# Handing out operand tiles and PSUM areas in strict rotation in a one-core attention and feed-forward kernel

## The chip, the cores and the metric

The kernel runs on one core of one Trainium2 chip. The metric is the device time of one execution in microseconds (us). The core's engines work side by side, each through its own queue of instructions in order, and wait for each other by semaphores: PE (TensorE, matrix products into PSUM), ACT (ScalarE), DVE (VectorE), POOL (GpSimd), and SP, which issues the transfers.

## What is computed

Two stages follow each other. The first is an attention through 49 agents: the agents attend to all keys and values, and each query attends to the agents. The second takes the 24960 resulting rows of 128 numbers through a feed-forward layer with 2048 hidden units and a clipped quadratic gate.

```python
def sm(a, b):
    s = scale * (a @ b.transpose(0, 2, 1))
    ...
    e = np.exp(s)
    return e / (e.sum(-1, keepdims=True) + 1e-09)
a2k = sm(agents, k)            # B = 2, N = 12480, C = 128, 49 agents
agent_v = a2k @ v
q2a = sm(q, agents)
x = q2a @ agent_v              # 24960 rows
...
h = x @ w_in                   # 128 -> 2048
g = np.where(h >= 1, h, np.where(h <= -1, 0.0, (h + 1) ** 2 / 4))
return g @ w_out               # 2048 -> 128
```

## The kernel before

The 24960 rows are cut into 49 tiles of 512. The 2048 hidden units are cut into eight pairs of 128-row blocks, so each tile has eight pairs, and a pair goes through these steps (function `pair`):

- `g1`: PE multiplies the tile's softmax weights `mt` (49 rows, kept as a high and a low part) with weights that already hold the agents' values times `w_in` (`w_hi`, `w_lo`), into a PSUM area `ph` of 128x1024. Six products (L1208).
- `relu` (L1216) and `square` (L1221): ACT writes `g = relu(0.5 h + 0.5)` from `ph`, then squares `g` in place.
- `gate` (L1224): DVE combines `g` and `ph` into the gated value, in place in `g`. After it `ph` is free.
- For six of the eight pairs `hi` (a rounded copy, `ghi`, L356 on POOL or L358 on DVE) and `lo` (the rest, `glo = g - ghi`, L1235, on POOL or DVE). After `lo` the tile `g` is free. Then PE adds `ghi` times `wo_hi` and `wo_lo`, and `glo` times `wo_hi`, into `total` (L1248).
- For the other two pairs PE multiplies `g` itself with `wo` (L1248, `total<-g,wo`), and `g` is free after that.

Between the pairs of a tile stand the query scores of a later tile (L1080, into a `ph` area), their softmax on DVE and ACT, the transposes of the result (L1127), and the output's evacuation (L354 `ot`, L1297) and store. Before the first tile the keys and values of the first batch are worked through. Those of the second batch ride along in tiles 3 to 23: their products (L381 keys, L389 values, L1016 weights) are put behind the query scores in the same `ph` area, and ACT and DVE then evacuate them (L354 `ks`, `w_hi`; L397 to L400 `acc`).

The order of the instructions on every engine is fixed when the kernel is built. A planner (class `Order`) places all steps by times written in tables (`TIMES`, `START`). It counts buffers (`BUFS`: five of `g`, five of `ghi`, five of `glo`, three of `ph`), but it does not choose which of them a step gets. The choice is made when a step's function runs and asks a pool for a tile:

```python
hip = ctx.enter_context(tc.tile_pool(name="hi", bufs=BUFS["hi"]))
...
def new_h():
    return psh.tile([128, 2, 512], F32, name="ph", tag="ph")
...
def wide(pool, name, dtype):
    return pool.tile([128, 2, T], dtype, name=name, tag=name)[:, :, 0:n]
```

All buffers of a kind share one tag, and the pool's allocator picks one for each new tile. The first instruction that writes a new tile then waits for the last users of the tile that had this buffer before. At the start some buffers of `g`, `ghi` and `glo` are lent to transfers of keys and values.

Of the kernel before, what the change touches and what calls it, by code (L numbers as in the profile page):

```python
# [13 lines left out]
F32 = mybir.dt.float32  # L14
F32R = mybir.dt.float32r
# [7 lines left out]
T = 512  # L23
# [32 lines left out]
    hi=(1.9175717, 2.5099120, None, 1.9817459, None, 2.5080745, 2.9293395, 2.4146834),  # L56
    lo=(2.3736696, 2.6831976, None, 1.9174717, None, 2.7685071, 2.6705867, 2.1491229),
# [16 lines left out]
BUFS = dict(k=4, v=4, q=4, qs=3, m=2, g=5, hi=5, lo=5, o=2, wf=2, h=3, d=2, ex=1, t0=1, t1=1)  # L74
# [172 lines left out]
def agent_attention_moe(  # L247
# [33 lines left out]
    small = ctx.enter_context(tc.tile_pool(name="small", bufs=BUFS["qs"]))  # L281
    qp = ctx.enter_context(tc.tile_pool(name="q", bufs=BUFS["q"]))
    mp = ctx.enter_context(tc.tile_pool(name="m", bufs=BUFS["m"]))
    gp = ctx.enter_context(tc.tile_pool(name="g", bufs=BUFS["g"]))
    hip = ctx.enter_context(tc.tile_pool(name="hi", bufs=BUFS["hi"]))
    lop = ctx.enter_context(tc.tile_pool(name="lo", bufs=BUFS["lo"]))
    op = ctx.enter_context(tc.tile_pool(name="o", bufs=BUFS["o"]))
    wfp = ctx.enter_context(tc.tile_pool(name="wf", bufs=BUFS["wf"]))
    dp = ctx.enter_context(tc.tile_pool(name="d", bufs=BUFS["d"]))
    dxp = ctx.enter_context(tc.tile_pool(name="ex", bufs=BUFS["ex"]))  # L290
    psh = ctx.enter_context(
        tc.tile_pool(name="psh", bufs=BUFS["h"], space=bass.MemoryType.PSUM)
    )
    psx = ctx.enter_context(tc.tile_pool(name="psx", bufs=1, space=bass.MemoryType.PSUM))

# [54 lines left out]
    dve, act, pool = nc.vector, nc.scalar, nc.gpsimd  # L350

    def copy(engine, out, in_):
# [4 lines left out]
        else:  # L357
            dve.tensor_copy(out, in_)  # L358

    def new_h():  # L360
        return psh.tile([128, 2, 512], F32, name="ph", tag="ph")

    PS = {}

# [168 lines left out]
    def keys_phase(b, keep, k_key, v_key, s_key, m_key, a_key, e_key, p_key=0.0, wait=None):  # L533
# [11 lines left out]
        for g in range(NG):  # L545
            lent = "g" if g % 2 and g < 2 * BUFS["g"] else "k"
            kb = [] if lent == "g" else [kbuf[keep.pop(0)]]

            def fn(o, e, g=g, kb=kb, h=slice(0, KG * SUB)):
                if not kb:  # L550
                    x = gp.tile([128, 2, T], F32, name="g", tag="g")
                    kb.append(x.rearrange("p c t -> p (c t)")[:, 0:KG * SUB])
                nc.sync.dma_start(out=kb[0][:, h], in_=kT[b, :, g * KG * SUB:][:, h])

            rest = []
            if g:
                LK[g] = load(128 * KG * SUB * 4, fn, (), k_key(g), (lent,))
            else:
                n, m = HALF * SUB, KG * SUB
                LK[g] = load(  # L560
                    128 * n * 4, lambda o, e, fn=fn: fn(o, e, h=slice(0, n)), (), k_key(g) - 1.0,
                    ("k",),
                )
                rest = [load(
                    128 * (m - n) * 4, lambda o, e, fn=fn: fn(o, e, h=slice(n, m)), (), k_key(g)
                )]

            def scores(o, e, g=g, kb=kb, lo=0, hi=HALF):
                if lo == 0:
                    area(o, ("k", b, g))  # L570
                ps = one(PS["k", b, g])


                for t in range(lo, hi):
                    columns(
                        ps[:, t * A:t * A + A2], kb[0][:, t * SUB:(t + 1) * SUB], agf[:, 0:A2]
                    )

            def scores2(o, e, scores=scores):
                scores(o, e, lo=HALF, hi=KG)  # L580

            def evac(o, e, g=g):
                copy(
                    e, ksf[:, g, 0:KG * A],
                    one(PS[("k", b, g)] if g else PS.pop(("k", b, g)))[:, 0:KG * A],
                )

            def gm(o, e, g=g):
                f = top.rearrange("p t a -> p (t a)")
                dve.tensor_tensor(  # L590
                    out=f, in0=one(PS.pop(("k", b, g)))[:, 0:KG * A],
                    in1=f if g > 1 else ksf[:, 0, 0:KG * A], op=ALU.max,
                )

            def gm2(o, e, g=g):
                dve.tensor_reduce(
                    out=pms[part(g)], in_=top.rearrange("p t a -> p a t"), axis=AX.X, op=ALU.max
                )

            x = add(("PE", 0.134 * HALF), scores, [LK[g], ld_ag], s_key(g))  # L600
            back = take(x)
            y = add(
                ("PE", 0.134 * (KG - HALF)), scores2, [x, *rest], s_key(g), (), ((lent, LK[g]),)
            )
            x.rows = y.rows = 2
            KE[g] = add(
                elementwise("evac", KG * A), evac, [y, *([wait[g]] if wait else [])], s_key(g) + 1, (),
                () if g else (back,),
            )
            if g:  # L610
                KX[g] = add(
                    ("DVE", 0.42), gm, [KE[g], *([KX[g - 1]] if g > 1 else [])], s_key(g) + 1.1, (),
                    (back,),
                )
            if g + 1 in (*first_of, NG):
                KX[g] = add(("DVE", 0.69), gm2, [KX[g]], s_key(g) + 1.2)

        mb_ops, rescale = [], None
        for i in range(len(first_of)):
# [36 lines left out]
            key = m_key if i + 1 == len(first_of) else p_key  # L656
            x = add(("PE", 0.1), m2, [KX[end]], key + 0.1)
            back = take(x)
            mx_op = x = add(("DVE", 0.2), m3, [x], key + 0.2)
            x = add(("DVE", 0.15, 1), m4, [x], key + 0.3)  # L660
# [7 lines left out]
        for g in range(NG):  # L668

            lent = ("hi", "lo")[g % 2] if b == 0 and g < NLENT else "v"  # L670
            vb = [vbuf[(b * NG + g - NLENT) % BUFS["v"]]] if lent == "v" else []
            s = ks[:, g, 0:KG, :]

            def fn(o, e, g=g, vb=vb, lent=lent):
                if not vb:
                    x = (hip if lent == "hi" else lop).tile(
                        [128, 2, T], F32R, name="g" + lent, tag="g" + lent
                    )
                    x = x.bitcast(F32).rearrange("p c t -> p (c t)")[:, 0:KG * (C + 1)]
                    vb.append(x.rearrange("p (t c) -> p t c", c=C + 1))  # L680
                nc.sync.dma_start(out=vb[0], in_=v[b, :, g * KG:(g + 1) * KG, :])

            LV[g] = load(SUB * KG * (C + 1) * 4, fn, (), v_key(g), (lent,))

            def sub(o, e, s=s, mb=mbs[part(g)]):
                (pool if e == "POOL" else dve).tensor_tensor(
                    out=s, in0=s, in1=mb.unsqueeze(1).to_broadcast([SUB, KG, A]),
                    op=ALU.subtract,
                )

            def exp(o, e, s=s):
                f = s.rearrange("p t a -> p (t a)")
                act.activation(out=f, in_=f, func=ACTF.Exp, scale=scale)

            g0 = first_of[part(g)]
            count = ((first_of + [NG])[part(g) + 1] - g0) * KG
            ps = total[:, 0, part(g) * 256:][:, 0:256]

            def av(o, e, g=g, vb=vb, g0=g0, count=count, ps=ps, lo=0, hi=HALF):
                beside(ps, g, vb[0], lo, hi, (g - g0) * KG, count)  # L700

            def av2(o, e, av=av):
                av(o, e, lo=HALF, hi=KG)

            k = a_key(g)
            x = add(elementwise("sub", KG * A), sub, [mb_ops[part(g)], KE[g]], e_key(g))
            x = add(("ACT", 0.39), exp, [x], e_key(g) + 0.5)
            x = add(
                ("PE", 0.125 * HALF), av, [x, LV[g], *av_ops[-1:]], k, () if g else ("t0",)
            )  # L710
            if not g:
                av_ops.append(x)
            x.rows = 2
            x = add(("PE", 0.125 * (KG - HALF)), av2, [x], k, (), ((lent, LV[g]),))
            x.rows = 2
            av_ops.append(x)
            if (g - g0 + 1) * KG == count:
                def plus(o, e, ps=ps, first=not part(g)):
                    join_halves(o, ps, first)

                if part(g):
                    last = add(("DVE", 0.2), rescale[1], [rescale[0], last], k + 0.9)
                last = add(
                    ("DVE", 0.45), plus, [x] + ([last] if part(g) else []), k + 1, (),
                    (("t0", av_ops[0]),) if part(g) else (),
                )
# [457 lines left out]
    def pair(j, p, w_ops, wo_op):  # L1184
        st = {}
# [9 lines left out]
        hi_e, lo_e = plan(HI_ENG, j)[p], plan(LO_ENG, j)[p]  # L1195
        n = width(j)

        def wide(pool, name, dtype):
            return pool.tile([128, 2, T], dtype, name=name, tag=name)[:, :, 0:n]

        def g1(o, e):
            st["h"] = new_h()
# [24 lines left out]
            )  # L1227

        def hi(o, e):
            st["hi"] = wide(hip, "ghi", F32R)  # L1230
            copy(e, st["hi"], st["g"])

        def lo(o, e):
            st["lo"] = wide(lop, "glo", F32R)
            (pool if e == "POOL" else dve).tensor_tensor(  # L1235
                out=st["lo"], in0=st["g"], in1=st["hi"].bitcast(F32), op=ALU.subtract
            )
# [202 lines left out]
```

## Time and profile before

| | |
|---|---|
| time, median of 3 runs | 1073.84 us (1072.96 to 1073.86) |
| time of the profiled execution | 1073.93 us |
| its span, first to last instruction | 1072.2 us |
| PE busy | 1003.1 us, 94% |
| DVE busy | 921.2 us, 86% |
| ACT busy | 903.0 us, 84% |
| POOL busy | 632.4 us, 59% |
| granted TensorE clock, mean over the span | 0.994 |

The profiled execution's time is 1.7 us above its span; that part lies outside the instructions. The engines' shares are means over a start of some 64 us, in which the transfers are busy, and 49 tiles of about 20 us each. A share below 100% says that an engine waited or had nothing to do, not which of the two; the views of waits and of the timeline tell that.

### The profile page before, as it was taken

The numbers are of one execution on the slowest core, as the hardware profiler recorded it, in microseconds if no ns is written. First come the engines' busy times: TensorE is split into PE (matmuls) and PEld (weight loads), VectorE is DVE, ScalarE is ACT, GpSimd is POOL, SyncE is SP. The second block draws the span as 40 slices with busy tenths as digits, with TensorE's granted clock in tenths as the row PEclk, the third lists the DMA queues.
The fourth block names the chain that finished last, engine by engine and source line by source line (L and its number), as shares of the span: only waits on it lengthen the run. The fifth ranks groups of instructions, "written<-read, shape, count | busy, mean of one in ns | idle before, by whom it ended". The sixth has DMA issues, their size and how long they took to land.

```text
span 1072.2 us, 22309 instructions
## 1 busy us (share of the span) xinstructions
PE 1003.1 (94%) x9092; PEld 775.6 (72%) x9092; DVE 921.2 (86%) x1128; ACT 903.0 (84%) x1001; POOL 632.4 (59%) x392
## 2 busy tenths in 40 slices
PE   5889999999999999999999999999999999999998
PEld 4766778767777777777778677777777776776766
DVE  6787888889989898888898898898898898898886
ACT  2467888899888888988898998988998998998986
POOL 3636646565665666465566566566566566566565
PEclk8999999999999999999999999999999999999999
DMA  9972110001122100000100100000000000000000
GB/s 339 377 243 68 39 31 28 24 30 38 48 65 90 58 28 31 21 31 21 31 29 23 31 31 21 30 31 21 30 31 21 30 31 21 28 21 11 11 20 19
DMA packets 23862, 57.06 MB, mean 53 GB/s; under 512 B 2896, under 2 KB 3280, under 8 KB 23760
## 3 DMA queue, kind: packets, MB, share of 16 engines
q1 hardware_dynamic: 23760, 55.63, 15.1%
q8 instruction: 72, 1.18, 0.5%
q14 instruction: 30, 0.25, 0.1%
HBM read 42.84 MB, written 12.78 MB: 52 GB/s over the span
## 4 chain that ended last, share of the span: by engine, by line
PE 65%; ACT 14%; DVE 10%; POOL 6%; issue 3%; DMA 1%; SPq 0%; DVEq 0%; POOLq 0%; ACTq 0%
PE total L1248 37%; PE ph L1208 22%; ACT g L1216 7%; DVE g L1224 6%; ACT g L1221 6%; POOL glo L1235 4%; POOL ghi L356 2%; PE ph L1127 1%; PE ph L381 1%; PE ph L389 1%; PE total L389 1%; DMA kbuf<-kT 1%; PE total L381 1%; PE ph L1080 0%; DVE qmx L1092 0%
## 5 line engine op out<-in xcount | busy, mean ns | idle before, releaser
L1235 POOL TENSOR_TENSOR glo<-g,ghi 128x1024 fp32r<-128x1024 f32 (+1 forms) x147 | 392.9, 2673 | 305.5 <-DVE ghi L358 300.7
L1224 DVE SCALAR_TENSOR_TENSOR g<-g,ph 128x1024 f32<-128x1024 f32 (+1 forms) x392 | 465.9, 1211 | 102.7 <-ACT g L1221 67.4
L1216 ACT ACTIVATE g<-ph,half 128x1024 f32<-128x1024 f32 (+1 forms) x392 | 427.9, 1104 | 81.9 <-POOL glo L1235 59.7
L1221 ACT ACTIVATE g<-g 128x1024 f32<-128x1024 f32 (+1 forms) x392 | 407.9, 1054 | 7.5
L1208 PE MATMUL ph<-mt,w_hi 49*128 49x512 f32 (+2 forms) x1600 | 287.0, 430 | 46.5 <-DVE g L1224 44.0
L356 POOL CAST ghi<-g 128x1024 fp32r<-128x1024 f32 (+1 forms) x196 | 200.4, 1037 | 88.8 <-DVE g L1224 83.2
L1208 PEld LDWEIGHTS ph<-mt,w_hi 49*128 49x128 f32 x1600 | 143.6, 186 | 115.6 <-DVE g L1224 54.4
L1235 DVE TENSOR_TENSOR glo<-g,ghi 128x1024 fp32r<-128x1024 f32 (+1 forms) x147 | 217.1, 1478 | 2.2 <-POOL ghi L356 1.8
L1248 PE MATMUL total<-ghi,wo_hi 64*128 64x512 f32 (+1 forms) x1176 | 190.8, 393 | 0.0
L1248 PE MATMUL total<-ghi,wo_lo 64*128 64x512 f32 (+1 forms) x1176 | 189.8, 391 | 0.0
L1248 PE MATMUL total<-g,wo 64*128 64x512 f32 (+1 forms) x784 | 184.8, 587 | 1.8 <-DVE top L888 1.5
L1208 PE MATMUL ph<-mt,w_lo 49*128 49x512 f32 (+2 forms) x800 | 162.2, 386 | 0.2 <-DVE w_lo L781 0.2
L1248 PE MATMUL total<-glo,wo_hi 64*128 64x512 f32 (+1 forms) x1176 | 154.5, 392 | 0.0
L1248 PEld LDWEIGHTS total<-ghi,wo_lo 64*128 64x128 f32 x1176 | 121.8, 185 | 15.1
L1248 PEld LDWEIGHTS total<-ghi,wo_hi 64*128 64x128 f32 x1176 | 121.7, 185 | 14.3
L1248 PEld LDWEIGHTS total<-glo,wo_hi 64*128 64x128 f32 x1176 | 118.7, 185 | 18.3
L1248 PEld LDWEIGHTS total<-g,wo 64*128 64x128 f32 x784 | 77.5, 185 | 54.0 <-issue 44.1
L1208 PEld LDWEIGHTS ph<-mt,w_lo 49*128 49x128 f32 x800 | 81.4, 184 | 11.4 <-DVE w_lo L781 0.9
L358 DVE CAST ghi<-g 128x1024 fp32r<-128x1024 f32 (+1 forms) x98 | 66.9, 683 | 0.1
L1080 PEld LDWEIGHTS ph<-ag,qt 128*64 128x64 f32 x780 | 27.1, 139 | 39.8 <-DVE g L1224 34.9
L354 ACT ACTIVATE ot<-total 128x512 f32<-128x512 f32 (+1 forms) x49 | 29.2, 595 | 30.6 <-PE total L1248 30.6
L1080 PE MATMUL ph<-ag,qt 128*64 128x49 f32 x780 | 33.2, 228 | 4.0 <-DMA qt<-qT 4.0
(111 smaller groups left out, 551.6 us busy)
## 6 DMA issues: line engine op xcount, KB each, us to landing
qt<-qT SPq DMA_DIRECT2D x48, 256.0 KB, 2.7
outT<-ot SPq DMA_DIRECT2D x48, 256.0 KB, 2.0
kbuf<-kT SPq DMA_DIRECT2D x22, 448.0 KB, 4.4
vbuf<-v_in SPq DMA_DIRECT2D x18, 451.5 KB, 4.3
ghi<-v_in SPq DMA_DIRECT2D x5, 451.5 KB, 7.5
glo<-v_in SPq DMA_DIRECT2D x5, 451.5 KB, 8.1
g<-kT SPq DMA_DIRECT2D x5, 448.0 KB, 9.6
raw<-w_in SPq DMA_DIRECT2D x4, 512.0 KB, 6.4
```

The lines of the kernel that those rows point to most:

```text
L354: act.activation(out=out, in_=in_, func=ACTF.Copy)
L356: pool.tensor_copy(out, in_)
L358: dve.tensor_copy(out, in_)
L381: nc.tensor.matmul(out=ps[c:c + 64], lhsT=lhsT[:, c:c + 64], rhs=rhs, start=True, stop=True)
L389: nc.tensor.matmul(out=ps[c:c + 64, 0:C + 1], lhsT=ksf[:, g, t * A:t * A + 64], rhs=vt[:, t, :], start=n + t < 2, stop=n + t >= m - 2,)
L1080: nc.tensor.matmul(out=ps[c, i * A:(i + 1) * A], lhsT=st["q"][:, i * 128:][:, c], rhs=ag[:, b, :], start=True, stop=True,)
L1208: nc.tensor.matmul(out=st["h"][:, c, lo:hi], lhsT=W[b][w][r, f:f + 128], rhs=M[j][r, x, lo:hi], start=(i == 0), stop=(i == 2),)
L1216: act.activation(out=st["g"], in_=st["h"][:, :, 0:n], func=ACTF.Relu, bias=half, scale=0.5)
L1221: act.activation(out=st["g"], in_=st["g"], func=ACTF.Square)
L1224: dve.scalar_tensor_tensor(out=st["g"], in0=st["g"], scalar=1.0, in1=st["h"][:, :, 0:n], op0=ALU.min, op1=ALU.max,)
L1235: (pool if e == "POOL" else dve).tensor_tensor(out=st["lo"], in0=st["g"], in1=st["hi"].bitcast(F32), op=ALU.subtract)
L1248: nc.tensor.matmul(out=total[:, i, 0:n], lhsT=w[r, f, :], rhs=x[r, c, :], start=begins, stop=LEFT[j] == 0,)
```

## The change

Every buffer of `g`, `ghi`, `glo` and `ph` gets a tag of its own with one buffer under it. A counter for each kind takes the tags in turn, so the n-th tile of a kind always gets buffer n modulo the number of buffers. The numbers of buffers, the planner and its tables are as before.

```diff
-    gp = ctx.enter_context(tc.tile_pool(name="g", bufs=BUFS["g"]))
-    hip = ctx.enter_context(tc.tile_pool(name="hi", bufs=BUFS["hi"]))
-    lop = ctx.enter_context(tc.tile_pool(name="lo", bufs=BUFS["lo"]))
+    gp = ctx.enter_context(tc.tile_pool(name="g", bufs=1))
+    hip = ctx.enter_context(tc.tile_pool(name="hi", bufs=1))
+    lop = ctx.enter_context(tc.tile_pool(name="lo", bufs=1))
...
-        tc.tile_pool(name="psh", bufs=BUFS["h"], space=bass.MemoryType.PSUM)
+        tc.tile_pool(name="psh", bufs=1, space=bass.MemoryType.PSUM)
...
+    RING = {}
+
+    def ring(pool, key, shape, dtype, name):
+
+        i = RING[key] = RING.get(key, -1) + 1
+        return pool.tile(shape, dtype, name=name, tag=f"{name}{i % BUFS[key]}")
+
     def new_h():
-        return psh.tile([128, 2, 512], F32, name="ph", tag="ph")
+        return ring(psh, "h", [128, 2, 512], F32, "ph")
...
-        def wide(pool, name, dtype):
-            return pool.tile([128, 2, T], dtype, name=name, tag=name)[:, :, 0:n]
+        def wide(pool, key, dtype):
+            name = key if key == "g" else "g" + key
+            return ring(pool, key, [128, 2, T], dtype, name)[:, :, 0:n]
...
-            st["hi"] = wide(hip, "ghi", F32R)
+            st["hi"] = wide(hip, "hi", F32R)
...
-            st["lo"] = wide(lop, "glo", F32R)
+            st["lo"] = wide(lop, "lo", F32R)
```

The built programs have the same working instructions in the same order on every engine. What differs is the buffers' addresses and with them the semaphores that instructions wait for. 241 of the 397 `g` tiles, 241 of 299 `ghi`, 96 of 299 `glo` and 6 of 512 `ph` follow another tile in their buffer than before; the six `ph` lie in the start and the first tile. A wait for a further semaphore stands in an instruction of its own ahead of the one that needs it; of these there are 96 more on ACT, 2 more on DVE, 1 more on POOL and 1 fewer on PE.

On ACT one tile in the middle of the program reads as follows before, with the numbers of the tiles and the engines whose semaphores each instruction waits for.

```order
L1216 ACTIVATE g_7045<-ph_7029,half_100 128x1024 [waits PE_49,Pool_49]
L1221 ACTIVATE g_7036<-g_7036 128x1024 [waits Activation_49]
L1221 ACTIVATE g_7045<-g_7045 128x1024 [waits Activation_49]
L1216 ACTIVATE g_7080<-ph_7050,half_100 128x1024 [waits DVE_49,PE_49,Pool_49]
L1216 ACTIVATE g_7101<-ph_7083,half_100 128x1024 [waits DVE_49,PE_49]
L1216 ACTIVATE g_7120<-ph_7105,half_100 128x1024 [waits PE_49]
L1216 ACTIVATE g_7151<-ph_7135,half_100 128x1024 [waits PE_49,Pool_49]
L1216 ACTIVATE g_7182<-ph_7164,half_100 128x1024 [waits PE_49]
```

The same instructions of the changed kernel (eight lines further down in the source):

```order
L1224 ACTIVATE g_7045<-ph_7029,half_100 128x1024 [waits PE_49,Pool_49]
L1229 ACTIVATE g_7036<-g_7036 128x1024 [waits Activation_49]
L1229 ACTIVATE g_7045<-g_7045 128x1024 [waits Activation_49]
L1224 ACTIVATE g_7080<-ph_7050,half_100 128x1024 [waits DVE_49,PE_49]
L1224 ACTIVATE g_7101<-ph_7083,half_100 128x1024 [waits DVE_49,PE_49,Pool_49]
L1224 ACTIVATE g_7120<-ph_7105,half_100 128x1024 [waits DVE_49,PE_49]
L1224 ACTIVATE g_7151<-ph_7135,half_100 128x1024 [waits DVE_49,PE_49]
L1224 ACTIVATE g_7182<-ph_7164,half_100 128x1024 [waits PE_49,Pool_49]
```

The wait for POOL has moved from the relu of `g_7080` to the next one, of `g_7101`: it is the wait for POOL's `lo` that reads the earlier tile `g_6955`, whose buffer goes to `g_7101` now. `g_7080` gets the buffer of `g_6924` instead, which the product `total<-g,wo` reads last. `g_7120` and `g_7182` wait for one engine more.

On POOL the same tile before:

```order
L356 CAST ghi_7027<-g_6981 128x1024 [waits DVE_49,Pool_49]
L356 CAST ghi_7043<-g_6955 128x1024 [waits PE_49]
L1235 TENSOR_TENSOR glo_7060<-g_6955,ghi_7043 128x1024 [waits PE_49,Pool_49]
L1235 TENSOR_TENSOR glo_7113<-g_7045,ghi_7103 128x1024 [waits DVE_49,PE_49]
L356 CAST ghi_7132<-g_7080 128x1024 [waits DVE_49,PE_49]
L356 CAST ghi_7144<-g_7101 128x1024 [waits DVE_49]
```

and with the change:

```order
L356 CAST ghi_7027<-g_6981 128x1024 [waits DVE_49,PE_49,Pool_49]
L356 CAST ghi_7043<-g_6955 128x1024 [waits Pool_49]
L1243 TENSOR_TENSOR glo_7060<-g_6955,ghi_7043 128x1024 [waits PE_49,Pool_49]
L1243 TENSOR_TENSOR glo_7113<-g_7045,ghi_7103 128x1024 [waits DVE_49]
L356 CAST ghi_7132<-g_7080 128x1024 [waits DVE_49,PE_49]
L356 CAST ghi_7144<-g_7101 128x1024 [waits DVE_49,PE_49]
```

The waits for PE (for products that read the buffer's earlier tile) have moved among the copies and the `lo` steps; the order has not.

## Rows read from the trace of the kernel before

**Rows 1.** The page's part 4: the chain that ended last, shares by engine.

```profile
PE 65%; ACT 14%; DVE 10%; POOL 6%; issue 3%; DMA 1%; SPq 0%; DVEq 0%; POOLq 0%; ACTq 0%
```

**Rows 2.** Waits, whole span: who waited for whom, us in total, times, longest.

```profile
ACT g L1216 <- POOL glo L1235: 59.7, 49, 2.9
PE ph L1208 <- DVE g L1224: 44.0, 54, 1.3
```

**Rows 3.** Windows, twenty tiles: length, busy us of PE, PEld, DVE, ACT, POOL, clock.

```profile
612.12:1012.22 400.10, 376.41 (x3197) 288.05 (x3198) 352.08 (x401) 357.58 (x381) 242.16 (x140) 1.00 0.08 25
```

**Rows 4.** Timeline of ACT, one tile: start, length, instruction, idle before and releaser.

```profile
603.32 2.01 ACT L1221 ACTIVATE g<-g 128x1024 f32<-128x1024 f32 x2
606.51 1.12 ACT L1216 ACTIVATE g<-ph,half 128x1024 f32<-128x1024 f32 x1 [1.18 <-POOL glo L1235]
607.66 1.06 ACT L1221 ACTIVATE g<-g 128x1024 f32<-128x1024 f32 x1
608.63 1.10 ACT L1216 ACTIVATE g<-ph,half 128x1024 f32<-128x1024 f32 x1
609.75 1.06 ACT L1221 ACTIVATE g<-g 128x1024 f32<-128x1024 f32 x1
610.72 1.10 ACT L1216 ACTIVATE g<-ph,half 128x1024 f32<-128x1024 f32 x1
```

**Rows 5.** Timeline of POOL in the same tile.

```profile
603.21 3.27 POOL L1235 TENSOR_TENSOR glo<-g,ghi 128x1024 fp32r<-128x1024 f32 x1
608.20 2.37 POOL L1235 TENSOR_TENSOR glo<-g,ghi 128x1024 fp32r<-128x1024 f32 x1 [1.72 <-DVE ghi L358]
610.51 1.04 POOL L356 CAST ghi<-g 128x1024 fp32r<-128x1024 f32 x1
```

**Rows 6.** Timeline of PE in the same tile.

```profile
601.84 1.88 PE L1248 MATMUL total<-g,wo 64*128 64x512 f32 x8
604.03 0.39 PE L1208 MATMUL ph<-mt,w_lo 49*128 49x512 f32 x2
606.60 0.39 PE L1208 MATMUL ph<-mt,w_lo 49*128 49x512 f32 x2
610.28 0.67 PE L1080 MATMUL ph<-ag,qt 128*64 128x49 f32 x16
612.12 0.73 PE L1208 MATMUL ph<-mt,w_hi 49*128 49x512 f32 x4 [1.17 <-DVE g L1224]
```

**Rows 7.** Timeline of DVE in the same tile.

```profile
602.18 2.02 DVE L1235 TENSOR_TENSOR glo<-g,ghi 128x1024 fp32r<-128x1024 f32 x1
...
607.37 0.68 DVE L358 CAST ghi<-g 128x1024 fp32r<-128x1024 f32 x1
610.84 1.22 DVE L1224 SCALAR_TENSOR_TENSOR g<-g,ph 128x1024 f32<-128x1024 f32 x1 [0.81 <-ACT g L1221]
...
612.94 1.22 DVE L1224 SCALAR_TENSOR_TENSOR g<-g,ph 128x1024 f32<-128x1024 f32 x1 [0.60 <-ACT g L1221]
614.07 1.22 DVE L1235 TENSOR_TENSOR glo<-g,ghi 128x1024 fp32r<-128x1024 f32 x1
```

**Rows 8.** Timeline, all engines, a tile in which keys ride along.

```profile
134.29 1.06 ACT L1221 ACTIVATE g<-g 128x1024 f32<-128x1024 f32 x1
135.26 0.44 ACT L354 ACTIVATE ks<-ph 128x343 f32<-128x343 f32 x1
137.37 0.73 PE L1208 MATMUL ph<-mt,w_hi 49*128 49x512 f32 x4 [0.44 <-DVE g L1224]
```

**Rows 9.** The chain of work that ended last, in time order, a tile with two value rides.

```profile
319.44 1.78 PE ph L389 x28
...
321.25 0.29 DVE acc L399
```

**Rows 10.** Waits in the stretch 300 to 411 us.

```profile
PE ph L1208 <- DVE g L1224: 3.3, 5, 0.7
```

**Rows 11.** Waits in the stretch 60 to 86 us.

```profile
PE ph L1208 <- DVE g L1224: 1.1, 2, 0.8
```

More of the change, by code (lines that the diff above doesn't have):

```diff
@@ L550, in fn @@
                 if not kb:
-                    x = gp.tile([128, 2, T], F32, name="g", tag="g")
+                    x = ring(gp, "g", [128, 2, T], F32, "g")
                     kb.append(x.rearrange("p c t -> p (c t)")[:, 0:KG * SUB])
@@ L675, in fn @@
                 if not vb:
-                    x = (hip if lent == "hi" else lop).tile(
-                        [128, 2, T], F32R, name="g" + lent, tag="g" + lent
+                    x = ring(
+                        hip if lent == "hi" else lop, lent, [128, 2, T], F32R, "g" + lent
                     )
```

## The prediction

> **What bounds the kernel now.** I first read the chain that ended last: PE holds 65% of it, but ACT, DVE and POOL hold 30% between them [rows 1], so PE is not simply saturated. The waits of the whole span name two that belong together. ACT's relu waits 59.7 us for POOL's `lo` (L1235), 49 times, and PE's first product of a pair waits 44.0 us for DVE's gate, 54 times [rows 2]: about once a tile each. The windows give their size: over twenty tiles without riders PE is busy 376.41 of 400.10 us, 18.82 of 20.0 a tile; ACT is busy 17.88 a tile, DVE 17.60 and POOL 12.11 [rows 3]. PE therefore idles 1.18 us in every such tile, and it has the most work.
>
> The timeline of one tile shows how one wait makes the other. I call the relu at 606.51 A and the next one, at 608.63, B. ACT is free at 605.33, when its second square ends, but A starts at 606.51, after 1.18 us of waiting for POOL [rows 4]; POOL's `lo` ran from 603.21 to 606.48 [rows 5]. Square A, relu B and square B follow without a gap, to 610.81 [rows 4]; DVE gates B from 610.84 to 612.06 [rows 7], which frees a `ph` area, and PE starts the next pair at 612.12 after 1.17 us of idling [rows 6]. A needs no result of that `lo`. It waits only because its buffer held the tile that this `lo` reads.
>
> **What the change does to this wait.** It adds no working instruction and moves none; only buffers and waits differ. After it A writes the buffer that PE's product with `wo` read last. That product runs from 601.84 to 603.72, and A's own `ph` is filled at 604.42 [rows 6]. Both are past when ACT is free at 605.33. B takes over the wait for POOL's `lo`. In the trace that `lo` ends at 606.48 and B starts at 608.63 [rows 4, 5], 2.15 us later.
>
> For every other tile that changed its buffer I set the end of the new predecessor's last user, in the trace of before, against the start of the new tile's first writer. None of the 584 comes late. The nearest are a key product in the start (0.01 us, worth a few hundredths of a us once), a POOL copy in the last tile (0.59) and a weight product in the start (0.93); in the steady tiles the margins are 2.1 us or more. So the change costs nothing by a late buffer and frees one wait a tile.
>
> **How far the freed time carries.** The two squares run 603.32 to 605.33, and instructions that don't wait start some 0.09 us before the one ahead has ended (relu B at 608.63, square A's end at 608.72) [rows 4]. So A starts at about 605.24, 1.27 us earlier. Relu B moves to 607.36: its `ph` is filled at 606.99 [rows 6] and the `lo` ended at 606.48 [rows 5], margins of 0.37 and 0.88. Square B then ends at 609.54. DVE ends its cast at 608.05 and needs 1.22 for gate A, to about 609.2 [rows 7], so gate B runs 609.57 to 610.79. PE, 0.06 after that, could start at 610.85. It is busy with query scores until 610.95 [rows 6]. The idle time is gone, with 0.1 us to spare, and PE becomes the bound: 18.82 a tile in place of 20.0.
>
> What follows in the tile keeps its distance to PE. Gate at 612.94 waited for ACT [rows 7] and moves by the same 1.27, a little more than PE's 1.17. ACT then is busy 17.88 of 18.82, DVE 17.60: both still fit, though barely.
>
> **Where it carries nothing, and the sum.** The term is PE's wait for the gate, 44.0 us [rows 2]. From it I take two pieces that have another cause:
> - 3.3 us between 300 and 411 us [rows 10]. Six tiles there carry two value products each. PE's value products end at 321.22, DVE adds them to `acc` from 321.25 on [rows 9], and the gate stands behind these additions on DVE. A starts earlier there too, but nothing waits for it.
> - 1.1 us between 60 and 86 us [rows 11], ahead of the first such A.
>
> In tiles where keys ride, PE idles twice, and the 44.0 holds both. The second gap, 0.44 at 137.37, hangs on ACT's evacuation `ks` at 135.26, which stands behind a square that started at 134.29 [rows 8]; that square is later on A's chain and moves by about 1 us. The weight riders have the same shape.
>
> 44.0 − 3.3 − 1.1 = 39.6 us. The profiled execution took 1073.93 us, 0.09 above the median, so 1073.93 − 39.6 = 1034.3. Small gaps will be left where the order at the end differs, so I round up to **1035 us**, 3.6% faster. If all of the 44.0 went, it would be 1030; that is the near end. The far end of the same mechanism is half of it back, 1054.
>
> **The added waits.** ACT gets 96 more wait instructions, two a tile (the orders above). The nearest row: relu B waits for two engines before the change and starts 0.09 us before square A's end; the relu at 610.72 waits for one and starts 0.09 before its predecessor's end, 610.81 [rows 4]. A satisfied wait costs nothing while ACT is busy, so I take nothing. From above it is bounded by the 0.02 to 0.03 us between a release and the start behind it (606.48 and 606.51 [rows 4, 5]): 96 × 0.03 = 2.9 us if all of it were exposed. On the stretch from A to B the number of waits is unchanged: one leaves A, one joins B.
>
> **The rivals.**
> - *The port takes it back.* DVE's `lo` takes 1.22 us at 614.07 and 2.02 at 602.18; POOL's takes 2.37 at 608.20 and 3.27 at 603.21, which is 2.37 counted from the end of DVE's long one, about 604.2 [rows 5, 7]. So the two hold each other up where they meet. After the change DVE's `lo` of 614.07 would start at 612.80. POOL's copy of A still starts at 610.51 behind its `lo`, and the copy of B right behind it, from 611.53 to 612.58 [rows 5]: 0.22 us ahead. If they met, DVE would lose 0.80 (2.02 − 1.22) in each of 43 tiles, 34 us, and the time would be 1069. DVE isn't the bound, so a part of it would not reach PE; with half of it, 1052. The Trainium skill says the same of this pair ("SBUF — State Buffer", the section on the engine and DMA sides of SBUF): a GpSimd instruction and a DVE one with two SBUF inputs take the shared port pair in turn, and the loser blocks for the whole instruction; this case's 2.02 against 1.22 agrees.
> - *Nothing moves,* 1074. The same gap in each tile could be for want of a sixth `g` buffer, which another order of the same five doesn't cure. It holds if no free buffer stands ready at 605.33. The trace has one, free since 603.72 [rows 6]. The Trainium skill ("Perfetto Trace Analysis", Optimization Strategy) reads consistent bubbles as possibly too few buffers; by that alone the time would stay.
> - *Slower: the wait is worse at B.* ACT works in order, so if POOL's `lo` ended after 608.63, B and all behind it would start later than before. The `lo` would have to end 2.15 us later than it does. One more `lo` of 2.37 ahead of it on POOL would do: 608.85, 0.22 late in each of 49 tiles, 11 us, 1085. Against it: no POOL instruction moves, and POOL is busy only 12.11 of 20 us [rows 3, 5].
>
> **Chances and range.** The forecast (1030 to 1043) 0.74; part of it taken back by the port, ACT or DVE (1043 to 1070) 0.16; no change 0.05; slower 0.05. A difference within 0.2% (about 2 us) can't be told from none here. So faster 0.90, same 0.05, slower 0.05. The range goes from 1029, a little under all of the 44.0, to 1050, a part of the second case, and holds a bit over 8 in 10.
>
> **What the profile of the changed kernel would show.** The wait of ACT's relu for POOL's `lo`, 59.7 us, falls to under 10. PE's wait for the gate falls from 44.0 to about 5, most of it between 300 and 400 us. Twenty late tiles take some 377 to 381 us, PE busy for all but a few of them. Shorter tiles with PE still idle would say that the next wait is ACT or DVE; DVE's `lo` with a longer mean, that it is the port. The granted clock, 1.00 in the steady tiles [rows 3], should stay. The prediction is wrong if A's gap goes and PE's stays: then B, or DVE's order around it, waits for something I took to be early.

## The result, and the profile of the changed kernel

The changed kernel takes 1028.3 us (median of four runs, 1027.95 to 1029.34) against 1073.85 us beside it; the ratio is 0.958 (95% interval 0.956 to 0.959). That is 45.5 us faster. The prediction said 39, and its range ended at 1029, 0.7 us too early. Direction, mechanism and place were right. One term of the sum, the price of PE's stops, was sized too small, and some smaller gains outside it stood at nothing.

The profiled execution took 1028.29 us with a span of 1026.5 us. Its page begins with the busy time of the engines, and its part 4 is the chain that ended last:

```profile
PE 997.7 (97%) x9092; PEld 761.7 (74%) x9092; DVE 917.9 (89%) x1128; ACT 901.9 (88%) x1001; POOL 631.3 (62%) x392
...
PE 92%; DVE 5%; ACT 1%; issue 1%; DMA 1%; SPq 0%; DVEq 0%; ACTq 0%
```

PE's share of the chain has gone from 65% to 92%, and POOL has left it [rows 1]. The waits over the whole span (who waited for whom, us in total, times, longest) have these rows for ACT's relu and PE's gate wait:

```profile
ACT g L1224 <- PE ph L1216: 33.3, 59, 2.0
...
PE ph L1216 <- DVE g L1232: 4.7, 8, 0.8
```

The relu's 59.7 us of waiting for POOL are gone: no such row is left. It now waits for PE, the engine with the most work. PE's wait for the gate fell from 44.0 to 4.7 us [rows 2]. All but 0.3 of what is left lies where the prediction had left it, six tiles with value products and the stretch before the first A. The same view from 290 to 400 us, and from 60 to 86 us:

```profile
PE ph L1216 <- DVE g L1232: 3.3, 5, 0.7
...
PE ph L1216 <- DVE g L1232: 1.1, 2, 0.8
```

These are the same 3.3 and 1.1 us as before [rows 10, 11]. The window of twenty late tiles that begins one tile earlier than that of before, at the same place in the tile (length, busy us of PE, PEld, DVE, ACT, POOL, clock, DMA share, GB/s):

```profile
574.54:949.53 374.99, 374.99 (x3204) 279.04 (x3200) 351.30 (x400) 356.53 (x381) 241.26 (x141) 1.00 0.09 28
```

PE has no idle time left in these tiles. They take 18.75 us each in place of 20.0 [rows 3], and the granted clock has stayed at 1.00.

One tile's timeline shows why. Here are ACT, then POOL, then PE one tile earlier (start, length, engine, instruction, idle before and releaser):

```profile
585.69 2.00 ACT L1229 ACTIVATE g<-g 128x1024 f32<-128x1024 f32 x2
587.59 1.11 ACT L1224 ACTIVATE g<-ph,half 128x1024 f32<-128x1024 f32 x1
588.73 1.06 ACT L1229 ACTIVATE g<-g 128x1024 f32<-128x1024 f32 x1
589.70 1.10 ACT L1224 ACTIVATE g<-ph,half 128x1024 f32<-128x1024 f32 x1
...
585.65 3.28 POOL L1243 TENSOR_TENSOR glo<-g,ghi 128x1024 fp32r<-128x1024 f32 x1
...
573.94 0.67 PE L1087 MATMUL ph<-ag,qt 128*64 128x49 f32 x16
574.54 0.73 PE L1216 MATMUL ph<-mt,w_hi 49*128 49x512 f32 x4
```

A starts at 587.59, 0.10 us before the second square's end (587.69), while POOL's `lo` still runs until 588.93. Before, A stood idle for 1.18 us until this `lo` had ended [rows 4, 5]. B, which has the wait for this `lo` now, starts at 589.70, 0.77 us after its end. And PE's first product of the pair behind the query scores starts 0.60 us after they start; before it was 1.84 (612.12 − 610.28 [rows 6]).

### The profile page after: what moved, and what is told of

It is laid out like the page before. It is cut to its first block, busy times and chain, and to the rows that moved or that the text cites. A ratio compares the mean times of both kernels' runs of the same rounds, so it can differ in the third digit from the quotient of the medians.

```text
span 1026.5 us, 22407 instructions
## 1 busy us (share of the span) xinstructions
PE 997.7 (97%) x9092; PEld 761.7 (74%) x9092; DVE 917.9 (89%) x1128; ACT 901.9 (88%) x1001; POOL 631.3 (62%) x392
## 3 DMA queue, kind: packets, MB, share of 16 engines
q8 instruction: 72, 1.18, 0.5%
## 4 chain that ended last, share of the span: by engine, by line
PE 92%; DVE 5%; ACT 1%; issue 1%; DMA 1%; SPq 0%; DVEq 0%; ACTq 0%
PE total L1256 55%; PE ph L1216 27%; PE ph L1087 3%; PE ph L388 2%; PE ph L1134 2%; DVE g L1232 1%; PE ph L396 1%; PE total L396 1%; DMA kbuf<-kT 1%; PE total L388 1%; PE ph L1023 0%; DVE dhi L463 0%; DVE acc L407 0%; DVE top L597 0%; DVE acc L406 0%
## 5 line engine op out<-in xcount | busy, mean ns | idle before, releaser
L356 POOL CAST ghi<-g 128x1024 fp32r<-128x1024 f32 (+1 forms) x196 | 197.9, 1039 | 66.5 <-DVE g L1232 60.3
L1243 DVE TENSOR_TENSOR glo<-g,ghi 128x1024 fp32r<-128x1024 f32 (+1 forms) x147 | 216.8, 1476 | 4.3 <-POOL ghi L356 2.9
L1256 PEld LDWEIGHTS total<-ghi,wo_lo 64*128 64x128 f32 x1176 | 118.4, 185 | 18.5
L1256 PEld LDWEIGHTS total<-glo,wo_hi 64*128 64x128 f32 x1176 | 116.0, 185 | 21.2
L1256 PEld LDWEIGHTS total<-ghi,wo_hi 64*128 64x128 f32 x1176 | 118.2, 185 | 17.8
L1099 DVE TENSOR_REDUCE qmx<-ph 128x4 f32<-128x196 f32 (+1 forms) x49 | 17.6, 360 | 23.4 <-ACT ks L354 9.2
```

The source lines that it names most:

```text
L356: pool.tensor_copy(out, in_)
L1243: (pool if e == "POOL" else dve).tensor_tensor(out=st["lo"], in0=st["g"], in1=st["hi"].bitcast(F32), op=ALU.subtract)
L1256: nc.tensor.matmul(out=total[:, i, 0:n], lhsT=w[r, f, :], rhs=x[r, c, :], start=begins, stop=LEFT[j] == 0,)
```

## The experiments

All times are medians; the ratio is to runs of the kernel before on the same chip, whose medians were 1073.53 to 1073.69 us. "A tile" is the time from one A to the next, as a mean over the same twenty late tiles of each kernel (tile 25 to 45, counted from 0), read from ACT's timeline. It was 20.00 before and 18.75 with the change.

| kernel | time, us | ratio (95% interval) | a tile, us |
|---|---|---|---|
| only `g` rotates | 1028.75 | 0.9583 (0.957 to 0.9596) | 18.74 |
| all but `g` rotate | 1074.76 | 1.0015 (1.0006 to 1.0024) | 20.05 |
| full rotation, A and B exchanged | 1076.8 | 1.0032 (1.002 to 1.0044) | 20.12 |
| the same from tile 25 on | 1060.21 | 0.9874 (0.9861 to 0.9888) | 20.11 |
| only `g` rotates, A and B exchanged | 1075.46 | 1.0015 (1.0006 to 1.0024) | 20.08 |
| changed kernel, less PE work | 1026.98 | 0.9565 (0.9551 to 0.9579) | 18.73 |
| kernel before, less PE work | 1073.06 | 0.9996 (0.9987 to 1.0006) | 20.01 |
| changed kernel, less ACT work | 1028.02 | 0.9574 (0.9561 to 0.9588) | 18.74 |
| changed kernel, less PE, less ACT (B) | 1024.16 | 0.9538 (0.9525 to 0.9551) | 18.66 |
| changed kernel, less PE, less ACT (another pair) | 1026.71 | 0.9564 (0.955 to 0.9579) | 18.73 |

The theory was the prediction's: the gain is the wait for POOL's `lo` that goes from A to B. The rivals: the gain comes from the rotated copies or PSUM areas; or from rotation as such, whichever tile gets whose buffer.

### Only `g` rotates, and all but `g` rotate

```diff
     def ring(pool, key, shape, dtype, name):
+        if key != "g":
+            return pool.tile(shape, dtype, name=name, tag=name)
```

(and its mirror, with `key == "g"`; the pools that don't rotate have their `BUFS` back)

> Only the g tiles rotate; ghi, glo and ph are handed out by the pool as before. If the whole gain is relu A's wait for POOL's lo, that wait is gone here too and the time is that of the changed kernel, 1028 us (1027 to 1030). Rival: the rotation of ghi and glo brings part of it (the 5 to 6 us by which the gain went past my sum); then 1033 to 1034.

> ghi, glo and ph rotate; g is handed out by the pool as before. If only the g buffers matter, relu A waits 59 to 60 us for POOL's lo in total as before and the time is that of before, 1074 us (1072.5 to 1075). Rival, ghi and glo bring 5 to 6 us: 1068 to 1069.

The rotation of `g` alone gives the whole gain. The other three without it give none; they cost 1.2 us. The relu's wait is back there:

```profile
ACT g L1226 <- POOL glo L1245: 61.2, 49, 2.9
```

### The full rotation with the buffers of A and B exchanged

```diff
         i = RING[key] = RING.get(key, -1) + 1
+        r = i - BUFS["g"]
+        if key == "g" and r >= 7 and r % 8 in (7, 0):
+            i += 1 if r % 8 == 7 else -1
```

> The changed kernel, but relu A and relu B of each tile exchange their g buffers, so A waits for POOL's lo again; everything else still rotates. If A's wait is all of it, and each stop of PE costs a little more than the idle time shown for it, the time goes back to that of before, 1072 to 1074.5 us. Rival, a stop costs just the idle time shown and the rest of the gain comes from elsewhere: 1028 + 40 = 1068. Rival, it is the rotation as such and not this one buffer: it stays near 1028.

Every other tile keeps its rotation; only the two `g` tiles of A and B trade buffers, so that A waits for POOL's `lo` again. All of the gain is gone. So the gain is the place of this one wait; rotation as such gives nothing. The time is 3 us above that of the kernel before, which no theory had expected. The next edit but one takes that up. The relu's wait here:

```profile
ACT g L1227 <- POOL glo L1246: 62.8, 49, 2.9
```

### The same exchange, in the later half alone

The edit is the same with `r >= 207`.

> As the kernel with A and B exchanged, but only from tile 26 on, some 22 tiles that have no riders and idle 1.18 us each on PE before. If a stop costs start to start 1.25 us, as the period of these tiles says (20.00 and 18.75): 1028.3 + 22 x 1.25 = 1055.8. Rival, it costs the idle time shown, 1.18: 1054.2. Rival, most of the gain lies in the first half: under 1045.

The waits came as expected, 24 of them:

```profile
ACT g L1227 <- POOL glo L1246: 30.7, 24, 1.5
```

They cost 1060.21 − 1028.3 = 31.9 us, 1.33 each. The expectation had counted 22 of them at 1.25 each, from start to start, and came out 4.4 us short: 2.5 for the two further waits, 1.9 because each cost 0.08 more. The rival that priced them at the idle time shown, 1.18, was further off. Of the 1.33, 1.26 is the difference of a tile between the kernel before and the changed one (20.005 − 18.749). The other 0.07 belongs to the added cost that the full exchange shows too (20.12 against 20.00).

### Only `g` rotates, A and B exchanged

The exchange above, put into the kernel in which only `g` rotates.

> Only g rotates, and A and B exchange their buffers in every tile; the copies, the lo tiles and the PSUM areas come from the pools as before. The full rotation with the same exchange took 1076.8, 3 us above the kernel before. If those 3 us come from the waits that the rotated ghi, glo and ph buffers add on the stretch that bounds it, this kernel takes 1073 to 1074.5 with late tiles of 20.00 to 20.02 us. If the exchange itself costs them (further waits on the relus), it takes 1076 to 1077 with late tiles of 20.06 to 20.09. Half of each gives 1075.

It came out between the two, so both parts cost something, and they add up: a tile is 0.08 longer than before here and 0.04 longer with all but `g` rotated, and 0.12 longer with both. The first part can be read at two relus that follow B. In the kernel before, the one at 633.20 waits for PE and POOL, the one at 635.31 for PE alone; here the one at 613.49 waits for DVE and PE, the one at 615.72 for PE and POOL. Each starts when PE has filled its `ph`. The timelines of before, then of this kernel, with the last products into that `ph` ahead of each relu:

```profile
632.70 0.40 PE L1208 MATMUL ph<-mt,w_lo 49*128 49x512 f32 x2
633.20 1.12 ACT L1216 ACTIVATE g<-ph,half 128x1024 f32<-128x1024 f32 x1 [0.29 <-POOL ghi L356]
634.85 0.43 PE L1208 MATMUL ph<-mt,w_lo 49*128 49x512 f32 x2
635.31 1.12 ACT L1216 ACTIVATE g<-ph,half 128x1024 f32<-128x1024 f32 x1
```

```profile
613.05 0.39 PE L1221 MATMUL ph<-mt,w_lo 49*128 49x512 f32 x2
613.49 1.12 ACT L1229 ACTIVATE g<-ph,half 128x1024 f32<-128x1024 f32 x1 [0.22 <-PE ph L1221]
615.21 0.41 PE L1221 MATMUL ph<-mt,w_lo 49*128 49x512 f32 x2
615.72 1.12 ACT L1229 ACTIVATE g<-ph,half 128x1024 f32<-128x1024 f32 x1
```

With PE and POOL to wait for, the relu starts 0.10 us after PE's last product (633.20 after 633.10; 615.72 after 615.62). With PE alone, or with DVE and PE, it starts 0.03 to 0.05 after (635.31 after 635.28; 613.49 after 613.44). In the exchanged kernel the slow pair of waits has moved from the earlier relu to the later one. The later relu then starts 2.23 us behind the earlier one in place of 2.11; the earlier one has gained 0.06 of these 0.12, so some 0.06 stays, most of the 0.08 found. The later relu does not wait for work of POOL: on this kernel's POOL timeline the last `lo` ahead of 615.72 ended at 610.90 and the last copy at 613.53. Nor does the earlier one of before, though its row names a POOL copy, which ended at 633.18: where all but `g` rotate, the same relu starts 0.10 us after PE's product as well, at 612.90, and there the copy ran until 612.96. Over twenty late tiles the medians are 0.10 for the relus with PE and POOL, in each of the seven kernels from before to this one, and 0.04 for the others that start on PE's end. The traces also show which wait stands where. With PE and POOL, the wait for PE stands in the instruction of its own ahead of the relu; that one ends 0.05 to 0.06 after PE's product, and the relu starts 0.05 behind it. With PE alone or with DVE and PE, the wait for PE stands in the relu itself.

For the second part, POOL's copy behind the gate (the cast that leads to the `lo` that A waits for) starts 0.159 us after the gate's end where `ghi` rotates and has three engines to wait for, and 0.133 after it in the kernel before, with two: medians over twenty late tiles. With the full exchange it is 0.159 again, with only `g` rotated and exchanged 0.133. That is 0.026 of the 0.04 us a tile; the rest was not traced.

### Less PE work, in the changed kernel and in that of before

The products of `glo` are left out for one of the six pairs, four matmuls, some 0.47 us a tile.

```diff
         def g2l(o, e):
+            if p == 0:
+                return
             product([(wo_hi, 2 * p + c, st["lo"], c) for c in range(2)])
```

> The changed kernel without the product of glo with wo_hi for the first of the eight pairs: four matmuls of some 0.117 us less on PE in each tile, 0.47 us x 49 = 23 us. If PE bounds the changed kernel and ACT and DVE still have room, all of it comes back: 1005 us. Rival, ACT (17.9 us busy a tile) or DVE (17.6) is as near the bound as PE: 1015 to 1025.

> The kernel before without the same product: four matmuls less on PE in each tile. If the loop through POOL's lo, relu A, relu B and the gate sets the period of the tiles without riders, PE's lighter load gives little: 1065 to 1074 us. Rival, PE bounds the kernel before as well: 23 us less, 1051.

Before, the work left out buys nothing: PE waits 59.2 us for the gate in place of 44.0.

```profile
PE ph L1208 <- DVE g L1224: 59.2, 85, 1.3
```

So PE's amount of work did not bound the kernel before, as the prediction read it. In the changed kernel it buys 1.3 us of the 23, less than either expectation, and a late tile stays at 18.73. That speaks against PE as the only bound. PE now waits for a gate once in each tile. Its product there, one tile earlier; then ACT, that gate on DVE and the product behind it:

```profile
614.36 0.73 PE L1216 MATMUL ph<-mt,w_hi 49*128 49x512 f32 x4 [0.16 <-DVE g L1232]
...
621.38 2.12 ACT L1224 ACTIVATE g<-ph,half 128x1024 f32<-128x1024 f32 x2
623.39 2.01 ACT L1229 ACTIVATE g<-g 128x1024 f32<-128x1024 f32 x2
625.29 1.11 ACT L1224 ACTIVATE g<-ph,half 128x1024 f32<-128x1024 f32 x1
...
630.63 1.06 ACT L1229 ACTIVATE g<-g 128x1024 f32<-128x1024 f32 x1
631.72 1.22 DVE L1232 SCALAR_TENSOR_TENSOR g<-g,ph 128x1024 f32<-128x1024 f32 x1 [0.27 <-ACT g L1229]
633.09 0.73 PE L1216 MATMUL ph<-mt,w_hi 49*128 49x512 f32 x4 [0.21 <-DVE g L1232]
```

A is the relu at 625.29 here; B is the one at 627.40. From 614.36 PE works without a stop until it has filled the `ph` of the relu at 621.38, 0.04 us ahead of it. From there ACT works without a stop, through A and B, to the end of the square at 631.69. The gate behind that square ends at 632.94, and PE's product starts 0.15 later. This second row of work, 7.0 us of PE, 10.3 of ACT and 1.4 of the gate and the start behind it, makes 18.73 us from one such product to the next, as long as a tile of the changed kernel. The product that was left out stood just ahead of the one that waits, outside this row. POOL is not in it: its `lo` ends at 626.63, and B starts behind its neighbour on ACT.

### Less ACT work, alone and with less PE work

The square of B's tile is left out (another pair's in the third kernel).

```diff
         def square(o, e):
+            if p == 3:
+                return
             act.activation(out=st["g"], in_=st["g"], func=ACTF.Square)
```

> The changed kernel without the square of relu B's tile (1.06 us of ACT in each of 49 tiles; the gate reads the unsquared value). If PE bounds the steady tiles, their period stays at 18.73 and the time at 1027 to 1028.5, with the rider tiles up to 10 us shorter where ACT's chain bounds them. If a loop through ACT bounds them and PE doesn't, the period falls by 0.3 to 1.0 and the time to 995 to 1015.

> The changed kernel without one pair's lo product (0.47 us of PE a tile) and without the square of relu B's tile (1.06 us of ACT a tile). If PE and a loop through this stretch of ACT bound the steady tiles together, each alone at 18.73, the period falls here, to 18.2 to 18.4, and the time by some 10 to 20 us, to 1007 to 1018, though without the PE products alone it fell by 1.3 only. If the second loop runs elsewhere (DVE and POOL alone), the period stays at 18.73 and the time at 1025 to 1027.

> As the kernel without one lo product and without the square of relu B's tile, but the square left out is that of another pair, later in the tile and not between A and the gate of B. If the second loop is ACT's whole row of instructions, this shortens the tile as much as the other one does (18.2 to 18.4, 1007 to 1018). If only the stretch from A to the gate of B is on that loop, the period stays at 18.7 and the time at 1025 to 1027.

With 1.06 us less of ACT's work and all of PE's, a tile stays at 18.74: PE alone makes that length, as the prediction says. With less of both it falls, but to 18.66 and not to 18.2 to 18.4, so the expectation's size was wrong. The square of another pair changes nothing (18.73), so the second row of work is not ACT's whole row; that square belongs to the relu at 615.41 above, outside the row. And a third row is only 0.09 shorter than a tile. ACT in the kernel with less of both:

```profile
612.32 1.12 ACT L1224 ACTIVATE g<-ph,half 128x1024 f32<-128x1024 f32 x1 [1.01 <-PE ph L1216]
613.47 1.06 ACT L1231 ACTIVATE g<-g 128x1024 f32<-128x1024 f32 x1
...
615.68 1.05 ACT L1231 ACTIVATE g<-g 128x1024 f32<-128x1024 f32 x1
616.63 1.10 ACT L1224 ACTIVATE g<-ph,half 128x1024 f32<-128x1024 f32 x1
617.77 1.06 ACT L1231 ACTIVATE g<-g 128x1024 f32<-128x1024 f32 x1
```

and the chain of the same kernel:

```profile
600.20 1.23 DVE g L1234
601.43 0.04 issue
601.47 0.96 PE ph L1216 x5
...
618.86 1.23 DVE g L1234
620.09 0.04 issue
620.14 0.96 PE ph L1216 x5
```

PE works without a stop from 601.47 until it has filled, at 612.27, the `ph` of the relu at 612.32. From there ACT has no pause to the end of the square at 618.83, then the gate takes until 620.08, and only then is a `ph` free for the product at 620.14. The chain puts a product of PE ahead of the relu at 616.63, but this relu starts 0.10 before the square ahead of it has ended (616.73), so it waited for ACT alone. The product that was left out stood among PE's products from 612.12 on, beside ACT's part of this row, and B's square stood beside PE's part, so leaving them out can't shorten this row.

## Why the prediction was right, and where its size was off

**The wait and its place.** Right. The exchange of two buffers brings all of the 45.5 us back, and the rotation of `g` alone gives it.

**How far the freed time carries.** Right in kind: the gaps in tiles without riders and with key riders went, those in the value tiles stayed with the same 3.3 us, and 1.1 us stayed ahead of the first A. Of the predicted 39.6 us of idle time at this wait, 44.0 − 4.7 = 39.3 went.

**The term that failed.** It is the first term of the sum, "PE's wait for the gate, 44.0 us", taken as the whole price of these stops. The wait counts the idle time between the modelled end of one product and the start of the next. Without a stop, the next product starts before that end: the query scores at 573.94 are shown until 574.61, and the product behind them starts at 574.54. So the stop at 612.12, shown as 1.17, cost 1.84 − 0.60 = 1.24. Set side by side in order, the starts of PE's records in the two traces show where the time went. Between the first record and the last they differ by 45.6 us. The 46 products at which such a stop went hold 42.9 of it: 3.5 more than the 39.4 of idle time that went there, 0.075 for each. PE's busy time shows the same thing: it fell by 5.4 us, 1003.1 to 997.7, though PE does the same work, and these 3.5 are part of it. The other 2.7 us were in no term of the sum. Of them, 0.7 lies in the first 20 us, where the granted clock was 0.74 (a mean of its two levels, 2.4 and 1.2 GHz) before and 1.00 (2.4 GHz throughout) after in the two profiled executions; no run ties that to the change. Some 0.6 lies at four first products between 447 and 511 us, whose idle time before, 0.07 to 0.13 each, the view of waits doesn't list. Some 0.8 lies between 1020 and 1060 us, at the end, and the rest in small steps; their cause stays open. The rounding up from 1034.3 to 1035 went the wrong way besides. The late tiles show it without any sum: predicted 18.82 for a tile, "in place of 20.0", found 18.75, because the 18.82 was PE's busy time with the stops' overlap counted in.

**The range.** Its near end, 1029, was "a little under all of the 44.0", so it rested on the same term, as the view shows it, and fell with it. From start to start the same stops give 1073.93 − 42.9 = 1031.0, and with the two pieces of 3.3 and 1.1 us in it a near end of 1026.6, below the time measured.

**"PE becomes the bound … both still fit, though barely."** Half right. PE alone makes the 18.75 (less ACT work changes nothing), but a row of work that passes from PE through ACT and DVE's gate back to PE makes 18.73 on its own. The busy times, 17.88 and 17.60 of 18.82 a tile, didn't show that; it is a matter of the order, not of an engine's load.

**The added waits.** "A satisfied wait costs nothing while ACT is busy" held with the change, where PE bounds the tile. The bound of 0.02 to 0.03 us for an exposed one was too low for ACT: a relu that had POOL to wait for, too, started about 0.06 later. A third wait at POOL's copy cost 0.026, within the bound; a second one cost more, 0.07: another copy of POOL, which waits for DVE alone in the kernel before, starts 0.064 us after the gate there, and 0.131 where `ghi` rotates and `g` doesn't and it waits for PE, too (medians of twenty late tiles). The kernels in which such waits lie on the bounding stretch lost 1.2 us (all but `g` rotate), 1.8 (only `g`, exchanged) and 3.2 (full exchange).

**The rivals.** The port took nothing back. After POOL's copies (574.00, 2.03) DVE's `lo` starts at 576.33 and takes 1.22, some 0.3 us clear of them, where the prediction had 0.22; DVE's `lo` has a mean of 1476 ns with the change:

```profile
L1243 DVE TENSOR_TENSOR glo<-g,ghi 128x1024 fp32r<-128x1024 f32 (+1 forms) x147 | 216.8, 1476 | 4.3 <-POOL ghi L356 2.9
```

The long ones are still there (2.02 where they meet POOL's copies), 47 against 48 before; that they fit the rule on the shared port of the Trainium skill ("SBUF — State Buffer", SBUF: two separate sides) stands as the prediction said. Counted from the end of DVE's long one at 604.20, though, POOL's `lo` took 2.28, not 2.37 [rows 5, 7]. "Nothing moves" fell: the gap was in every tile and five buffers were enough without it, so the reading of consistent bubbles as possibly too few buffers in the Trainium skill ("Perfetto Trace Analysis", Optimization Strategy) does not hold for this gap, and the measurement decides. "Slower at B" fell with B's margin of 0.77 us, against 0.88 read ahead of the change.

## What to carry to other kernels

When an in-order engine waits for a reader that its own data doesn't need, look at which buffer the new tile was given: another one of the same set may have been free for over a microsecond, and the choice costs nothing. Price a stop of PE from start to start, against the same pair of products at a place without a stop; the idle time as shown was 0.075 us too short for each here. After the bound has moved, take a little work from the new bound before working on it: here 23 us less of PE's work bought 1.3, since two other rows of work were within 0.1 us of it.

## What the runs showed of the hardware

A relu that waits for PE and, beside it, for a POOL instruction that ended microseconds ago starts 0.10 us after PE's last product; one that waits for PE alone, or for DVE and PE, 0.04 after (medians). The records of the wait instructions fit one reading: what counts is whether the wait that ends last stands in the working instruction or in the wait instruction ahead of it. POOL's copy starts 0.06 after the gate with the wait for it in the copy, 0.13 with that wait ahead of the copy, and 0.16 with a second one there. PE's first product of a pair starts 0.06 after the gate in the kernel before, at 612.12, and 0.15 after it at the product at 633.09 with less PE work, where the wait for DVE stands ahead. No run exchanged the two waits of one instruction, so this stays a reading. While the engine has other work to do up to the start, none of it is seen: with the change B waits for three engines and starts 0.09 before the square ahead of it has ended (589.70, 589.79).
